# q and k of eight attention blocks read as pairs of tokens, in an attention and expert kernel on one core

## The chip, the cores and the metric

The kernel runs on one core of a Trainium2 chip. The core has a matrix engine (TensorE, PE in the profile; its weight loads are PEld), a vector engine (VectorE, DVE), an activation engine (ScalarE, ACT), a general engine (GpSimd, POOL), and SyncE (SP), which here only issues DMAs. Sixteen DMA engines move data between the device memory and the core's on-chip memory (SBUF); matrix results land in a second memory (PSUM), which DMAs don't reach. The metric is device time in microseconds of one launch. Before the change it was 397.56 us, the median of three runs (396.06 to 397.76).

## The reference

The kernel computes sliding-window attention with four sink tokens, and feeds the result to a layer of four experts that are all evaluated and mixed by given shares.

```python
# q, k, v: (4, 8, 768, 64) float32; n_sink = 4, window = 128
scores = q @ k.transpose / sqrt(64)
keep = (key < n_sink) | ((query - key >= 0) & (query - key < window))
a = softmax(where(keep, scores, -1e9))
x = (a @ v).transpose(0, 2, 1, 3).reshape(3072, 512)

p = domain_probs / (domain_probs.sum(-1) + 1e-9)        # (3072, 4), the shares
for e in range(4):                                      # w1: (4, 512, 1024), w2: (4, 1024, 512)
    out += p[:, e:e+1] * (relu(x @ w1[e]) @ w2[e])      # out: (3072, 512) float32
```

## The kernel before

Tokens are handled in 24 blocks of 128, each with all eight heads of one of the four sequences. Blocks 0 to 3 are the first 128 tokens of the four sequences, blocks 4 to 7 their second 128 tokens, and blocks 8 to 23 the rest, sequence by sequence. In the code a block is `u`; `place(u)` gives its sequence and its place in it.

A block is loaded by three DMAs on SP's queue (q, k, v; `load`, line 209). A DMA for 128 tokens and eight heads has 1024 pieces of 64 float32 numbers, 256 bytes each. Each of q, k and v has two buffers, so the load of block u waits until block u - 2 has been read. GpSimd casts what has landed to bf16 (`cast`, line 217). For blocks 0 to 7 TensorE transposes q and k (`pe_tr`, line 278); for blocks 0 and 1 it transposes the float32 numbers as they landed, without a cast. ScalarE or VectorE copies the transposed q and k out of PSUM (`q_out`, `k_out`). Later blocks are transposed by DMA. Keys of blocks 0 to 7 lie in the tile that all keys of a sequence share (sequences 0 and 1), or in a side tile `kside` (sequences 2 and 3), out of which `move_keys` copies them later. `sink_keys` copies the four sink keys of each sequence to tiles of their own, `skd`.

Then follow, for each block: the scores (`scores`, line 330: one matmul a head, 128 queries by the 128 keys of the block before and its own 128 keys, or its own alone in blocks 0 to 3); mask, scale and minimum on VectorE (line 353); exponentials on ScalarE (line 361); the transpose of the weights (tile `tra`, copied to `AT`); the product with v (`op`); the division by the sum (`xn`); and the transpose of the result to `xT`, the experts' input.

The experts' work is cut into items of tokens times one expert: first two items of 256 tokens (blocks 0 and 1, then 2 and 3) with expert 0, then items of 512 tokens. An item's first product goes to `hpsum` (line 494), passes a relu (`ht`) and its second product goes to `mopsum` (line 520). The result, times the token's share, is added into `out_sb`, and SP stores it (line 569). The eight weight tiles are loaded in pieces of 2 MB of float32 that the DMA casts to bf16, on GpSimd's own DMA queue (lines 228 and 231); the table `w_at` says behind which cast GpSimd issues each.

The shares are loaded as 24 rows of 2 KB, one row for each tile of 128 tokens, into `dp_nat` (`load_small`, line 234), the third DMA on SP's queue. TensorE turns them (`turn_shares`, tile `trs`, line 241), and VectorE divides them by their sums.

The order of all this is written out by a planner inside the kernel, which runs when the program is built. Each step is a node with engines and costs, dependencies and a due time (tables `starts` and `MOVED`); the planner always takes the step that can begin first and among these the one due first, and writes it to its engine. Each engine then works through its instructions strictly in that order, and waits where one is not ready. Where the planner sees TensorE without work in the first stage, it writes filler matmuls (`keep_busy`, line 478). SP's loads keep a fixed order. Each DMA of SP raises one of eight semaphores in turn, and so waits until the DMA eight places before it has landed.

Of the kernel before, what the change touches and what calls it, by code (L numbers as in the profile page):

```python
# [16 lines left out]
def kernel(  # L17
# [48 lines left out]
    UF = 2  # L66

# [23 lines left out]
    def tile_of(u):  # L91
# [17 lines left out]
    kside = {  # L109
        b: resid.tile([P, NHP, 2, P], BF16, name=f"kside{b}", tag=f"kside{b}") for b in range(2, B)  # L110
    }
# [23 lines left out]
    def own_keys(m):  # L135

        nc.gpsimd.affine_select(
            out=m, in_=m, compare_op=ALU.is_ge, fill=MASKED,
            base=0, pattern=[[-1, P]], channel_multiplier=1,
        )  # L140

    def keys_before(m):

        nc.gpsimd.affine_select(
            out=m, in_=m, compare_op=ALU.is_gt, fill=MASKED,
            base=0, pattern=[[1, P]], channel_multiplier=-1,
        )
# [3 lines left out]
    own_keys(M0)  # L151
    nc.vector.memset(M0[:, 0:NSINK], 0.0)
    for m in (M1, M2):
        nc.vector.memset(m, 0.0)
        own_keys(m[:, 1])
        keys_before(m[:, 0])
# [22 lines left out]
    def weigh_sinks(eng, u):  # L179
# [3 lines left out]
        for r in range(NSINK):  # L183
            t = sv if r == 0 else at_sb.tile([P, H, D], FP32, name="svr", tag="svr", bufs=1)
            nc.gpsimd.tensor_mul(  # L185
                t, vsb[place(u)[0]][:, :, r], pr[:, :, r : r + 1].to_broadcast([P, H, D])
            )
            if r:
                nc.gpsimd.tensor_add(sv, sv, t)  # L189
# [19 lines left out]
    def load(eng, u, what):  # L209
        b, qb = place(u)  # L210
        t = resid.tile([P, H, D], FP32, name="raw" + what, tag="raw" + what, bufs=NRAW[what])
        nc.sync.dma_start(  # L212
            out=t, in_=src_of[what][b, :, qb * P : (qb + 1) * P, :].rearrange("h p d -> p h d")
        )
        raw[what, u] = t

    def cast(eng, u, what):
# [5 lines left out]
        else:  # L223
            nat[what, u] = resid.tile([P, H, D], BF16, name=what + "n", tag=what + "n", bufs=2)
            copy_on(eng, nat[what, u], t)
# [29 lines left out]
    def keys_of(b):  # L255
        if b not in kT:
            kT[b] = at_sb.tile([P, NHP, NQB, P], BF16, name="kT", tag="kT", bufs=2)
# [5 lines left out]
    def front_keys(b):  # L263
        return kside[b] if b in kside else keys_of(b)
# [6 lines left out]
    def dma_k(eng, u):  # L271
        b, qb = place(u)
        nc.sync.dma_start_transpose(
            out=keys_of(b)[:, :, qb],
# [3 lines left out]
    def pe_tr(eng, u, what):  # L278
        src = raw.pop((what, u)) if u < UF else nat.pop((what, u))
        ps = ps_s.tile([P, NHP, P], FP32 if u < UF else BF16, name="tr" + what, tag="s")  # L280
        for hp in range(NHP):
            nc.tensor.transpose(  # L282
                ps[:, hp], src[:, 2 * hp : 2 * hp + 2, :], identf if u < UF else ident
            )
# [5 lines left out]
    def k_out(eng, u):  # L290
        b, qb = place(u)
        copy_on(eng, front_keys(b)[:, :, qb], live.pop(("trk", u)))

    def move_keys(eng, b):
        copy_on(eng, keys_of(b)[:, :, 1], kside[b][:, :, 1])
# [34 lines left out]
    def scores(eng, u, g):  # L330

        b, qb = place(u)
        lo = 0 if qb else 1
        kt = front_keys(b) if u < UPS else keys_of(b)
        first = qb - 1 + lo
        sp = {}
        for h in groups_of(u)[g]:
            if h % 2 not in sp:
                sp[h % 2] = ps_s.tile([P, 2, 2, P], FP32, name="sp", tag="s")
            r = slice(h % 2 * D, (h % 2 + 1) * D)  # L340
            nc.tensor.matmul(  # L341
                sp[h % 2][:, h // 2 % 2, lo:2], lhsT=queries_of(u)[r, h // 2],
                rhs=kt[r, h // 2, first : qb + 1], start=True, stop=True,
            )
# [221 lines left out]
    def store(eng, i, sub):  # L566
        tok = items[i][0] + sub * P
        rt = tile_of(tok // P)
        nc.sync.dma_start(
            out=out[rt * P : (rt + 1) * P, :], in_=out_sb[tok // 512][:, (tok % 512) // P, :]  # L570
        )
# [32 lines left out]
    starts = [-11.6, -24.6, 21.4, 5.8, 41.4, 66.5, 75.8, 38.7, 5.1, 34.6, 6.6, 66.0, 99.7]  # L604
# [17 lines left out]
    for u in range(NU):  # L622
# [4 lines left out]
        for j, what in enumerate("qkv"):  # L627
            last = u - NRAW[what]
            free = ("cast", last, what)
            if last < UF and what != "v":  # L630
                free = ("tr" + what, last)
# [5 lines left out]
            if u - AHEAD >= UPA:  # L637
                deps.append((("begun", "da", u - AHEAD, 1), HOP))
            node(("load", u, what), {"SP": 0.5}, lambda eng, u=u, w=what: load(eng, u, w), deps,
                 S0 - 24.0 + 0.1 * j, dma=1.0 if u < 2 else 1.1)  # L640
            deps = [(("load", u, what), HOP)]
            if u < UF and what != "v":
                continue
# [5 lines left out]
            elif u >= UF + 2:  # L649
# [413 lines left out]
```

## Time and profile before

| | |
|---|---|
| median of three runs | 397.56 us |
| the profiled execution | 396.68 us |
| its span, first to last instruction | 395.0 us |
| TensorE busy | 388.4 us |
| VectorE, ScalarE, GpSimd busy | 218.7, 213.7, 181.6 us |
| first expert matmul | 24.49 us after the span's start |
| filler matmuls on TensorE | 69 |
| packets of SP's DMA queue | 142724, 44.11 MB |
| packets of GpSimd's DMA queue (the weights) | 6272, 8.39 MB |

All times of instructions count from the span's start. The time of an execution is a little longer than its span. An engine's busy time is the time in which it had an instruction under way; a group's row gives how many instructions of a kind there were and how long one took on average. Matmuls overlap, so the step from one matmul's start to the next one's is shorter than the time of one: 0.216 us for 512 columns at the full clock, where one takes 0.379. The granted clock is the share of TensorE's clock that the chip let through. The share of the DMA engines can exceed 1, because packets on one engine overlap.

### The profile page before, as it was taken

Reading aid. Unit: us, or ns where it says so; the run is one execution under the profiler, and the core shown is the slowest. Engines: PE = TensorE matmul, PEld = TensorE weight load, DVE = VectorE, ACT = ScalarE, POOL = GpSimd, SP = SyncE. Lnnn points to the kernel's source line nnn. Section 1 sums busy time; section 2 is a strip of 40 time slices with the busy share of each in tenths; the row PEclk is TensorE's granted clock in tenths of the full one; section 3 lists DMA queues with packets and bytes.
Section 4 is the critical chain, followed back from the end, with each engine's and each line's share of the span. In section 5 each row is a group of like instructions: output and inputs, shape, how many; then the busy total and the mean of one; then the engine's idle time right before and its main releaser. Section 6 shows DMA issues by size and latency. Waiting matters only on the chain.

```text
span 395.0 us, 7130 instructions
## 1 busy us (share of the span) xinstructions
PE 388.4 (98%) x2457; PEld 193.2 (49%) x2457; DVE 218.7 (55%) x694; ACT 213.7 (54%) x606; POOL 181.6 (46%) x208
## 2 busy tenths in 40 slices
PE   7999999999999999999999999999999999999996
PEld 5776555544544444444444444444444444444443
DVE  2970678887355984943787934838845223101223
ACT  5875777667374563854564855835654342344320
POOL 2710332047828658595586981695975200000000
PEclk9989999999999999999999999999999999999999
DMA  9999999779299898795886948984933000110002
GB/s 177 211 200 199 205 205 183 185 116 194 57 138 201 178 228 204 139 210 99 196 163 148 209 99 166 217 140 84 217 95 69 13 2 0 53 55 0 0 2 106
DMA packets 149031, 52.94 MB, mean 134 GB/s; under 512 B 135404, under 2 KB 143980, under 8 KB 148996
## 3 DMA queue, kind: packets, MB, share of 16 engines
q1 hardware_dynamic: 142724, 44.11, 55.2%
q0 software_dynamic: 6272, 8.39, 13.3%
q8 instruction: 19, 0.31, 0.3%
q14 instruction: 16, 0.13, 0.1%
HBM read 39.90 MB, written 6.29 MB: 117 GB/s over the span
## 4 chain that ended last, share of the span: by engine, by line
PE 95%; DVE 2%; DMA 1%; SPq 1%; issue 0%
PE hpsum L494 43%; PE mopsum L520 42%; PE sp L341 3%; PE op L420 3%; PE tra L399 2%; DMA rawq<-in_q_dram 1%; PE idle_out L481 1%; DVE SM L353 1%; PE trq L282 1%; PE trk L282 1%; PE trx L470 1%; PE lpsum L537 0%; SPq L212 0%; PE ss L305 0%; SPq L234 0%
## 5 line engine op out<-in xcount | busy, mean ns | idle before, releaser
L494 PE MATMUL hpsum<-xT,w 128*128 128x512 bf16 (+1 forms) x800 | 180.6, 372 | 0.1
L520 PE MATMUL mopsum<-w,ht 128*128 128x512 bf16 x760 | 172.5, 379 | 0.0
L508 ACT ACTIVATE ht<-hpsum 128x512 bf16<-128x512 f32 x157 | 92.4, 595 | 99.8 <-PE hpsum L494 68.6
L520 PEld LDWEIGHTS <-ht 128*128 128x128 bf16 x760 | 73.3, 98 | 85.9 <-issue 0.6
L494 PEld LDWEIGHTS <-w 128*128 128x128 bf16 x800 | 74.6, 98 | 81.8 <-issue 9.1
L361 ACT ACTIVATE A<-SM,negm 128x256 bf16<-128x256 f32 (+1 forms) x192 | 91.7, 480 | 20.3 <-DVE negm L353 14.9
L562 DVE SCALAR_TENSOR_TENSOR out_sb<-mopsum,shares,out_sb 128x512 f32<-128x512 f32 x71 | 53.0, 746 | 81.1 <-PE mopsum L520 80.3
L189 POOL TENSOR_TENSOR sv<-sv,svr 128x512 f32<-128x512 f32 x48 | 60.9, 1269 | 3.8
L353 DVE CUSTOM_DVE_ANT_0 SM<-sp,M,slow 128x256 f32<-128x256 f32 x128 | 54.4, 478 | 6.7 <-PE sp L341 6.7
L185 POOL TENSOR_TENSOR svr<-vsb,As 128x512 f32<-128x512 f32 x48 | 52.9, 1102 | 2.5
L361 ACT ACTIVATION_READ_ACCUMULATOR A<-SM,negm 128x1 f32 x192 | 36.2, 188 | 0.0
L506 DVE TENSOR_SCALAR ht<-hpsum 128x512 bf16<-128x512 f32 x35 | 24.0, 686 | 16.6 <-PE mopsum L520 16.1
L558 ACT ACTIVATE out_sb<-mopsum,shares 128x512 f32<-128x512 f32 x20 | 13.8, 688 | 33.8 <-PE mopsum L520 33.8
L185 POOL TENSOR_TENSOR sv<-vsb,As 128x512 f32<-128x512 f32 x16 | 17.2, 1077 | 30.8 <-ACT As L375 30.8
L199 POOL CAST qn<-rawq 128x512 bf16<-128x512 f32 x22 | 13.5, 614 | 36.5 <-DMA rawq<-in_q_dram 35.0
L199 POOL CAST kn<-rawk 128x512 bf16<-128x512 f32 x22 | 13.6, 617 | 21.5 <-DMA rawk<-in_k_dram 17.5
L353 DVE CUSTOM_DVE_ANT_0 SM<-sp,M 128x128 f32<-128x128 f32 (+1 forms) x64 | 19.3, 352 | 5.8 <-PE sp L341 5.5
L448 DVE TENSOR_TENSOR sv<-op,sv 128x512 f32<-128x512 f32 x16 | 10.9, 683 | 20.2 <-POOL sv L189 17.7
L199 POOL CAST vn<-rawv 128x512 bf16<-128x512 f32 x20 | 13.2, 662 | 15.4 <-DMA rawv<-in_v_dram 15.4
L420 PEld LDWEIGHTS <-AT 128*128 128x128 bf16 x352 | 13.9, 100 | 4.8 <-issue 0.2
L353 DVE DVE_READ_ACCUMULATOR2_ANT negm<- 128x1 f32 x192 | 15.8, 82 | 0.0
L420 PE MATMUL op<-vn,AT 128*128 128x64 bf16 x288 | 14.4, 196 | 0.0
(79 smaller groups left out, 197.9 us busy)
## 6 DMA issues: line engine op xcount, KB each, us to landing
w<-in_moe_w_dram POOLq DMA_DIRECT2D x8, 1024.0 KB, 11.4
rawq<-in_q_dram SPq DMA_DIRECT2D x24, 256.0 KB, 3.7
rawk<-in_k_dram SPq DMA_DIRECT2D x24, 256.0 KB, 5.0
rawv<-in_v_dram SPq DMA_DIRECT2D x24, 256.0 KB, 5.4
out_dram<-out_sb SPq DMA_DIRECT2D x23, 256.0 KB, 2.4
vsb<-in_v_dram SPq DMA_DIRECT2D x4, 1024.0 KB, 7.0
AT<-A SPq DMA_TRANSPOSE x32, 4.2
qT<-qn SPq DMA_TRANSPOSE x16, 2.5
```

The source lines that it names most:

```text
L185: nc.gpsimd.tensor_mul(t, vsb[place(u)[0]][:, :, r], pr[:, :, r : r + 1].to_broadcast([P, H, D]))
L189: nc.gpsimd.tensor_add(sv, sv, t)
L199: nc.gpsimd.tensor_copy(out=out, in_=in_)
L353: nc.vector.tensor_tensor_reduce(out=SM[:, h][part], in0=live.pop(("sp", u, h))[part], in1=masks[min(qb, 2)], scale=-scale, scalar=live["s ...
L361: nc.scalar.activation(out=Abuf[u % 2][:, 2 * h + lo : 2 * h + 2, :], in_=SM[:, h, lo:2], func=AF.Exp, scale=-1.0, bias=live["negm", u][:, ...
L420: nc.tensor.matmul(op[:, h], lhsT=at[:, 2 * h + i], rhs=vn[key][:, h, :], start=(i == blocks[0][0]), stop=(i == 1),)
L494: nc.tensor.matmul(ps[:, j * n : (j + 1) * n], lhsT=w1[e][:, db, fb * P : (fb + 1) * P], rhs=xT[t0 // 512][:, db, t0 % 512 : t0 % 512 + n] ...
L506: nc.vector.tensor_scalar_max(out=ht, in0=ps, scalar1=0.0)
L508: nc.scalar.activation(out=ht, in_=ps, func=AF.Relu)
L520: nc.tensor.matmul(ps, lhsT=hidden(i, fb, sub), rhs=w2[e][:, fb, :], start=(fb == 0), stop=(fb == NFB - 1),)
L558: nc.scalar.activation(out=dst, in_=ps, func=AF.Copy, scale=sc)
L562: nc.vector.scalar_tensor_tensor(out=dst, in0=ps, scalar=sc, in1=dst, op0=ALU.mult, op1=ALU.add)
```

## The change

Of blocks 0 to 7, q and k are read as pairs of tokens. Two tokens that follow each other in a sequence are 512 adjacent bytes for one head. A load is now two DMAs, one for heads 0 to 3 and one for heads 4 to 7, each of 64 token pairs times four heads: the pair's number and the group of heads give the partition, so that the first DMA fills the even partitions and the second the odd ones. v is read as before.

After the cast and the transpose, a head's 128 tokens lie in every second column of a tile of 256, first the even tokens and then the odd ones. Queries stay in this order: rows of a block are then tokens 0, 2, 4, ..., 1, 3, 5, .... Masks of these blocks are set up for it in two halves, stores are two DMAs of 64 rows each, and the shares of these eight tiles are read once more, in eight small DMAs, into the order of the rows. Keys are read in the order of the tokens, alternately out of the even and the odd half. All keys of blocks 0 to 7 stay in `kside`, now one tile for each sequence, and `move_keys` falls away. Where a block's keys lie in `kside`, or in `kside` and in the tile of the later keys, its scores take two matmuls of 128 keys for each head instead of one of 256.

Blocks 0 and 1 are now cast too, by VectorE, and no block is transposed in float32. The shares are loaded behind v of block 3. The table of the weights, the planner's due times and some of its costs are new, so that the order of the instructions changes on every engine: there are 105 fillers instead of 69, the shares are turned after the first 24 expert matmuls instead of before them, and in GpSimd's order the first three weight pieces are issued behind the casts of k of block 2 (two pieces) and of v of block 3.

```diff
     def load(eng, u, what):
...
+        from_ = src_of[what][b, :, qb * P : (qb + 1) * P, :]
+        if u < UPS and what != "v":
+            for g in range(2):
+                nc.sync.dma_start(
+                    out=t.rearrange("p (f j) d -> p f (j d)", j=2)[g::2, 0:NHP],
+                    in_=from_[g * NHP : (g + 1) * NHP].rearrange("f (p j) d -> p f (j d)", j=2),
+                )
+        else:
+            nc.sync.dma_start(out=t, in_=from_.rearrange("h p d -> p h d"))
...
     def cast(eng, u, what):
...
+            if u < UPS:
+                copy_on(
+                    eng, nat[what, u].rearrange("p (j f) d -> p f j d", j=2),
+                    t.rearrange("p (f j) d -> p f j d", j=2),
+                )
...
+    def load_pairs(eng):
+        for b in range(B):
+            for j in range(2):
+                nc.sync.dma_start(
+                    out=dp_nat[b * NQB : b * NQB + 2, j * D : (j + 1) * D],
+                    in_=moe_domain_probs[b * S : b * S + 2 * P].rearrange(
+                        "(t p j) e -> j t p e", t=2, j=2
+                    )[j],
+                )
...
+    def front_queries(u, h):
+        t = qTb[u % 2].rearrange("p (m j) c -> p m (j c)", j=2)
+        r = slice(h % 2 * D, (h % 2 + 1) * D)
+        return t[r, h % NHP // 2, h // NHP :: 2]
+
+    def front_keys(b, qb, h):
+        r = slice(h % 2 * D, (h % 2 + 1) * D)
+        return kside[b][r, h % NHP // 2, qb].rearrange("p (j c) -> p c j", j=2)[:, h // NHP :: 2]
...
     def sink_keys(eng, b):
         for c in range(2):
             r = slice(c * D, (c + 1) * D)
-            copy_on(eng, skd[b][r, :, c], front_keys(b)[r, :, 0, 0:NSINK])
+            for g in range(2):
+                copy_on(
+                    eng, skd[b][r, g * HG : (g + 1) * HG, c].rearrange("p m (j t) -> p m j t", j=2),
+                    kside[b][r, :, 0].rearrange("p m (j c) -> p m j c", j=2)[:, :, :, g : g + 3 : 2],
+                )
...
     def scores(eng, u, g):
         b, qb = place(u)
...
+        parts = [(0, 2)] if qb > 2 else [(0, 1), (1, 2)] if qb else [(1, 2)]
...
+            for a, z in parts:
+                if qb - 1 + a < 2:
+                    keys = front_keys(b, qb - 1 + a, h)
+                else:
+                    keys = keys_of(b)[r, h // 2, qb - 3 + a : qb - 3 + z]
+                nc.tensor.matmul(
+                    sp[h % 2][:, h // 2 % 2, a:z],
+                    lhsT=front_queries(u, h) if u < UPS else queries_of(u)[r, h // 2],
+                    rhs=keys, start=True, stop=True,
+                )
...
     def store(eng, i, sub):
...
+        for j in range(2):
+            nc.sync.dma_start(
+                out=rows.rearrange("(p j) d -> j p d", j=2)[j], in_=have[j * D : (j + 1) * D]
+            )
...
-            node(("cast", u, what), {"POOL": 0.56},
+            node(("cast", u, what), {"DVE": 0.42} if u < 2 and what != "v" else {"POOL": 0.62},
...
-    w_at = [(2, 'k'), (2, 'k'), (2, 'k'), (4, 'q'), (5, 'q'), (6, 'k'), (9, 'v'), (11, 'q')]
+    w_at = [(2, 'k'), (2, 'k'), (3, 'k'), (4, 'k'), (5, 'v'), (6, 'v'), (9, 'k'), (9, 'v')]
...
+    node(("pairs",), {"SP": 4.0}, load_pairs, [], 5.0, dma=0.9)
-    node(("trs",), {"PE": 0.46}, turn_shares, [(("small",), HOP), (("s", 3, 1), 0.0)], 9.0, "s")
+    node(("trs",), {"PE": 0.46}, turn_shares, on([("pairs",), ("s", 3, 3)]), 9.0, "s")
...
-        if u == 0:
-            loads.insert(2, ("small",))
+        if u == 3:
+            loads += [("small",), ("pairs",)]
```

More of the change, by code (lines that the diff above doesn't have):

```diff
@@ L64 @@
     UG = 4
-    UF = 2
     NVN = 4
@@ L108 @@
     skd = [resid.tile([P, NHP, 2, NSINK], BF16, name=f"skd{b}", tag=f"skd{b}") for b in range(B)]
-    kside = {
-        b: resid.tile([P, NHP, 2, P], BF16, name=f"kside{b}", tag=f"kside{b}") for b in range(2, B)
-    }
+    HG = H // NHP
+    kside = [
+        resid.tile([P, HG, 2, HG * P], BF16, name=f"kside{b}", tag=f"kside{b}") for b in range(B)
+    ]
     idle_in = consts.tile([P, P], BF16, name="idle_in")
@@ L278, in pe_tr @@
     def pe_tr(eng, u, what):
[L279 to L284, printed above, removed]
+        src = nat.pop((what, u))
+        ps = ps_s.tile([P, NHP, P], BF16, name="tr" + what, tag="s")
+        for j in range(2):
+            for m in range(HG):
+                i = j * HG + m
+                nc.tensor.transpose(ps[:, m * 2 + j], src[:, 2 * i : 2 * i + 2, :], ident)
         live["tr" + what, u] = ps
@@ L568, in store @@
         rt = tile_of(tok // P)
-        nc.sync.dma_start(
-            out=out[rt * P : (rt + 1) * P, :], in_=out_sb[tok // 512][:, (tok % 512) // P, :]
-        )
+        rows, have = out[rt * P : (rt + 1) * P, :], out_sb[tok // 512][:, (tok % 512) // P, :]
+        if tok // P >= UPS:
+            nc.sync.dma_start(out=rows, in_=have)
+            return
+        for j in range(2):
+            nc.sync.dma_start(
+                out=rows.rearrange("(p j) d -> j p d", j=2)[j], in_=have[j * D : (j + 1) * D]
+            )
     nodes = {}
@@ L674 @@
                 have.append((("dk", u - 1), HOP))
-            elif b >= 2:
-                node(("kc", b), {"POOL": 0.56, "ACT": 0.58}, lambda eng, b=b: move_keys(eng, b),
-                     kfree + on([("ko", B + b)]), S0 - 6.0)
-                have.append((("kc", b), HOP))
             else:
```

118 lines of the change are left out of this document (51 added, 67 removed).

## The prediction

> **What bounds the kernel now.** I read the page's busy times and the chain first, then busy times by stage, then the packets of the DMA queues by stage, then the timelines of PE and POOL.
>
> ```profile
> PE 388.4 (98%) x2457; PEld 193.2 (49%) x2457; DVE 218.7 (55%) x694; ACT 213.7 (54%) x606; POOL 181.6 (46%) x208
> PE 95%; DVE 2%; DMA 1%; SPq 1%; issue 0%
> ```
>
> TensorE is busy throughout, and the chain runs over it for 95% of the span. So an edit counts only as it moves the start of the steady stretch, adds matmul time, or makes PE wait.
>
> ```profile
> 5.00:10.00 5.00, 4.25 (x24) 2.88 (x23) 1.88 (x13) 3.59 (x15) 0.61 (x1) 1.00 1.33 221
> 15.00:20.00 5.00, 4.55 (x60) 3.61 (x57) 4.73 (x23) 4.14 (x22) 3.57 (x6) 1.00 1.17 204
> 20.00:25.00 5.00, 4.65 (x48) 3.52 (x49) 4.77 (x33) 4.89 (x25) 0.39 (x2) 0.80 1.17 199
> 30.00:35.00 5.00, 5.00 (x41) 3.77 (x39) 0.00 (x0) 2.98 (x5) 0.00 (x0) 1.00 1.13 203
> ```
>
> Columns: stage, its length, busy PE, PEld, DVE, ACT, POOL, granted clock, DMA share, GB/s. Until about 24 us the attention of blocks 0 to 3 runs: DVE is at 4.7 of 5 us, ACT at 4.1 to 4.9, the DMA engines are full. PE's busy time there holds 69 filler matmuls. From 24.5 us on PE has no gap.
>
> ```profile
> 22.74 0.67 PE L241 MATMUL trs<-identf,dp_nat 24*128 24x24 f32 x4
> 23.34 0.29 PE L481 MATMUL idle_out<-idle_in 128*128 128x128 bf16 x1
> ...
> 13.09 0.61 POOL L199 CAST kn<-rawk 128x512 bf16<-128x512 f32 x1 [0.44 <-DMA rawk<-in_k_dram]
> 13.64 0.94 POOL L228 DMA_DIRECT2D w<-in_moe_w_dram  x1
> ```
>
> The turn of the shares (trs) stands in PE's order just before the first expert matmul (24.49 us). The weights start behind the cast of k of block 2.
>
> ```profile
> q1 hardware_dynamic: 7808, 1.97, 131.4%
> ...
> q0 software_dynamic: 267, 0.54, 95.4%
> q1 hardware_dynamic: 265, 0.07, 17.4%
> ...
> q0 software_dynamic: 461, 0.47, 92.2%
> q1 hardware_dynamic: 458, 0.12, 29.5%
> ```
>
> These are queue lines (packets, MB, share) of 5 to 14 us, 30 to 33 us (first weights, 2 KB pieces) and 24 to 27 us (second weights, 1 KB). Alone, the loads move 868 packets of 256 B per us: 16 engines / 868 = 18.4 ns each on one engine, 1.18 us a load. Beside weights the two queues take **turns, packet for packet**: 267 to 265, 461 to 458. One turn of both costs an engine 48 us / 267 = 180 ns, or 48 / 461 = 104 ns. A small packet then waits for a big one each time.
>
> **The change, part by part.** All against the profiled execution, 396.68 us (span 395.0); it lies 0.9 below the median, 397.56, within the runs' 396.06 to 397.76.
>
> *Loads.* A q or k load becomes two DMAs of 256 packets of 512 B. The packet records have 27 ns for the 512 B pieces of the last stores, 18 for 256 B: 512 x 27 / 16 = 0.86 us against 1.18. Block 3's k, the eighth such load, landed at 16.6 us; 8 x 0.3 earlier, and 0.7 more for the share load that leaves the head of the queue, is 13.5. SP issues 20 DMAs for four blocks instead of 12. One with 128 rows took 0.33 to 0.57 us, a DMA transpose 1.2; I take 0.45, nearest in kind: 2.3 us a block, under the 2.9 of its transfers. At 1.2 SP would be the bound, 5 us a block, +7 in all.
>
> *Blocks 0 and 1.* Four casts on DVE replace float32 transposes. Four transposes took 1.09 us in float32 and 0.59 in bf16; the cast lies between 0.41 (DVE bf16 copy) and 0.69 (float32 to bf16); I take 0.42, since it reads SBUF. Per load that is nothing net on the chain, but DVE gets 1.7 us more; the copies out of bf16 take 0.42 there instead of 0.69. The sink-key copies double (0.41 to about 0.8 us a block; block 2's on ACT, the others on POOL). ACT's own front (32 exps at 0.39, seven copies, the sink keys: 17 us from 7.7 us) then ends about 24: ACT and not the loads sets the end, so the first expert matmul comes at about 24.0 instead of 24.5. Term: **-0.5** (from -3.1, if it followed block 3's k, to +1, if the 105 fillers, 36 more, run at the slow 0.107 us).
>
> *Scores.* 64 score matmuls of 256 columns in the steady stretch become 128 of 128 with two weight loads a head. Eight heads took 0.45 us from first start to last plus its pitch, two heads side by side. Half-width ones of one head cannot run side by side: five steps of 0.056 for four heads against 0.225. Eight blocks x 2 groups x 0.06 = **+1.0** (0.4 to 3.6, if none overlap). The moving keys are now read alternating between two runs 256 B apart; no row of before has such a read; bounds are 0 and a doubled 0.056 step. The Trainium skill ("SBUF — State Buffer", section on Door 1) says that reads crossing to a new 16-byte line each time pay a penalty, and these do; it gives no figure, and at double steps the sum would have +4.9 here instead of +1.0. I stay at 1.0, since no row shows the penalty.
>
> *Shares.* This is the large term. The share load (before: second on the queue, 24 rows of 2 KB) now follows block 3's v, and eight more DMAs rewrite parts of dp_nat. Each has 2 rows of 64 pieces of 16 B. They wait for the first one (same tile), and trs, in PE's order 2.84 us after the first expert matmul (sum of the pitches ahead of it), waits for all. An engine takes whole rows: the landing record of before's 24-row load has 12 arrivals, that of every 128-row load 16. Two rows thus use two engines at most, 64 packets on each, 512 for the eight. The Trainium skill ("DMA: Bandwidth & Descriptors", section on why a DMA increments its semaphore by 16) says the same: the largest count up to 16 that divides the slowest dimension, and always the lowest-numbered engines; the 12 of 24 rows agrees.
>
> Block 3's v lands near 14.6, so the pair loads start near 15 to 16. The weights come first: k of block 2 lands near 10.6, POOL has its sink copies and q's cast ahead of it and ends k's cast near 12.0, so w starts 1.6 us earlier than 13.64. In before three pieces went out back to back and the third landed at 36.4 us, 22.75 after the first issue; now 34.5, its last packet at 33.5. They are 32 + 64 + 32 turns per engine, some 120 of them after 16 us, and each lets one pair packet through. So at 33.5 two engines still hold 512 - 120 = 392. Alone each costs between 0 and 18.4 ns (the 256 B row): 0 to 7.2 us; I take 9 ns, half, since 16 B are less than 256: 3.6. Landing takes about 1 us more (first load: 3.3 us from issue, its packets done after 2.3). Landed: **38.1** (34.5 to 41.7). PE stands at trs from 24.0 + 2.84 = 26.8: **+11.3** (7.7 to 14.9). Everything on PE queues behind it; so do SP's next loads, since each waits for the eighth DMA before it to land. They then have no weights beside them and come 8 us or more before PE needs q of block 4 (8.5 us of expert work comes first), so I cost them nothing; if that cover fails, the trk of block 5 is late next, 18 us after trs.
>
> *Clock.* Before shows one spell at half clock: 0.80 and 0.86 over 20 to 30 us, 1.7 us lost. An idle PE of 11 us should bring one more: **+1.7** (0 to 3.4).
>
> *The rest.* Stores of eight tiles are cut in two: 8 more DMAs, 0.33 to 0.53 us each on SP, beside PE's steady work. Two key moves (0.6 us) go. POOL's casts keep 0.61. Three more mask steps (0.29 each) end before the first load lands. Nothing on the path; if SP were late, the AT transposes would be next.
>
> Sum: 396.7 - 0.5 + 1.0 + 11.3 + 1.7 = 410.2; against the median, half of the 0.9 added, **411**.
>
> **Rivals.**
> - *The pair loads are hidden and the front follows the loads.* If the sixteen engines shared the 1024 pieces, 64 each, they would be through at 16 + 24 turns of 180 ns + 40 of 104 = 24.5 us, landed before 26.8: no wait. Fourteen engines are the point from which this decides; the 12 arrivals speak against. With the first expert matmul 3.1 us sooner: 396.7 - 3.1 + 1.0 = 394.6. For it: DMA is full until 24 us. Against: DVE and ACT are at 4.7 and 4.1 of 5 us.
> - *Hidden, and ACT sets the front's end:* 396.7 - 0.5 + 1.0 = 397.2, no change that can be told.
> - *Hidden, but PE's new key reads run at half pace:* 396.7 - 0.5 + 4.9 = 401.1. Nothing in the profile speaks for or against.
>
> **Numbers.** Forecast 0.66, by the turns (two stretches, 1 to 1) and the 12 arrivals; first rival 0.10, second 0.13, third 0.11. Own range of the forecast: 405 (wait 8, no clock spell) to 417 (wait 15, clock 3.4, scores 2), the other terms as taken. To leave out no more than 2 in 10, the range goes down to 397, which takes in the third rival and half of the second: 397 to 418. About 0.5% (2 us) is what a measurement of this kernel tells from no change: faster 0.10, same 0.13, slower 0.77.
>
> **What the profile after will show.** PE idle of 8 to 15 us ending in trs, with dp_nat's DMA as its releaser, near 27 to 39 us; DMA share falling to a small part once the weights are through; the loads of block 4 issued late; a half-clock spell after 38 us; first expert matmul near 24; score steps of 0.056. Wrong would make it: dp_nat landed before 26 us (pieces over all engines, or queues that don't take turns), or weights that start after the pair loads.

## The result

The changed kernel takes 413.79 us, median of four runs (412.38 to 414.26), beside 396.81 (395.47 to 397.76, four runs) for the kernel before on the same chip. The ratio is 1.0419, 95% interval 1.0368 to 1.0471: slower by 17.0 us. Forecast were 411 us, 405 to 417 for the likeliest case, and 397 to 418 with the rivals. One execution of an experiment below (the turn put later) ran at a granted clock of 0.66 and took 575 us; it stands in no median here. The profiled execution took 414.26 us, its span is 412.5 us. The page's busy times and chain:

```profile
PE 390.0 (95%) x2515; PEld 196.6 (48%) x2557; DVE 206.5 (50%) x683; ACT 223.1 (54%) x620; POOL 180.9 (44%) x218
...
PE 88%; DMA 5%; SPq 4%; issue 1%; DVE 1%; ACT 0%; DVEq 0%; ACTq 0%
```

TensorE is still the bound, but 9% of the chain are now DMAs and SP's issue of them (before: 1% and 1%). PE's waits (tile and line, its releaser: us in all, times, longest) and the timelines of PE, SP and GpSimd say where:

```profile
PE trs L267 <- DMA dp_nat<-in_moe_domain_probs_dram: 10.9, 1, 10.9
PE hpsum L534 <- DMA xT<-xn: 1.5, 1, 1.5
```

```profile
25.68 1.04 PE L534 MATMUL hpsum<-xT,w 128*128 128x256 bf16 x8
...
39.91 0.64 PE L267 MATMUL trs<-identf,dp_nat 24*128 24x24 f32 x4 [10.88 <-DMA dp_nat<-in_moe_domain_probs_dram]
...
40.88 6.99 PE L534 MATMUL hpsum<-xT,w 128*128 128x256 bf16 x40
```

```profile
13.70 0.56 SPq L224 DMA_DIRECT2D rawv<-in_v_dram  x1
14.31 0.58 SPq L250 DMA_DIRECT2D dp_nat<-in_moe_domain_probs_dram  x1
27.33 10.43 SPq L257 DMA_DIRECT2D dp_nat<-in_moe_domain_probs_dram  x8
```

```profile
13.47 0.94 POOL L244 DMA_DIRECT2D w<-in_moe_w_dram  x1
...
26.95 0.61 POOL L203 CAST vn<-rawv 128x512 bf16<-128x512 f32 x1 [9.94 <-DMA rawv<-in_v_dram]
```

PE stood at the turn of the shares from 29.0 to 39.9 us, and started again at half clock (the stage's columns as in the prediction; the eighth number is the granted clock):

```profile
40.00:45.00 5.00, 5.00 (x28) 3.77 (x29) 1.00 (x4) 1.64 (x3) 2.66 (x4) 0.50 0.80 212
```

The 40 expert matmuls from 40.88 took 6.99 us; the first 23 of them stepped by 0.213 us, the 24th by 0.173, the others by 0.109. The pair loads were issued only from 27.33 us: v of block 3, which SP issued 0.2 us after GpSimd had issued the first weight piece, landed at 26.9, and the 24-row load behind it, for which the pair loads wait, at 27.3. The queues of 30 to 33 us, when PE waited (queue: packets, MB, share):

```profile
q0 software_dynamic: 271, 0.56, 103.8%
q1 hardware_dynamic: 35, 0.00, 1.6%
```

271 weight packets on sixteen engines are 16.9 for each. 35 pair packets on two engines are 17.5 for each: turns, packet for packet, on two engines. Until 34.8 us the pair packets went two to four in 0.2 us, from then on up to 68, so that from there these two engines seem to have had no weight packets left (the third piece landed at 36.5). 912 of the 1024 pair packets, 456 an engine, were still to go, and went in 4.3 us: 253 from 35 to 36 us, then some 200 per us, as fast as SP issued them (128 in 0.64 us).

The score matmuls between 52 and 75 us that read keys out of `kside` (ns min/median/max, start of the first and last, form), first before (blocks 6 and 7), then after (blocks 4 to 6, without the last two matmuls):

```profile
L341 PE MATMUL sp<-kside,qT x16: 266/269/280, 61.2 to 70.2; 64*128 64x256 bf16 x16
```

```profile
L380 PE MATMUL sp<-kside,qT x46: 296/298/304, 56.0 to 75.0; 64*128 64x128 bf16 x46
```

A matmul of half the keys takes longer than one of all had. By the starts in the trace, two heads side by side step, from pair to pair, by 0.137 us for 128 alternating keys; in block 8, whose second half comes out of the tile of the later keys, they step by 0.057 for 128 keys in a row. (From the second head of a pair to the next pair it is 0.130 and 0.050.)

The books, span against span (17.5 us): the first expert matmul comes 1.2 later (25.68, before 24.49); the wait 10.9; score matmuls, start to next start, 15.65 after and 11.50 before, 4.15; half-clock steps 2.7 after and 1.0 before, 1.7; the wait for xT 1.5; the turns, now behind the first expert matmul, 0.6. That is 20.1. Against it, the 512-column matmuls of the experts lost less than before: over 0.216 us for each, those of the first products took 3.3 us before and 1.2 after (the wait for xT aside), those of the second 0.6 and 0.1, 2.6 less in all (with 42 matmuls whose records are missing after counted at 0.216): 17.5. Why they lost less is not shown.

### The profile page after: what moved, and what is told of

The parts are those of the page before. It is cut to its first block, busy times and chain, and to the rows that moved or that the text cites. A ratio compares the mean times of both kernels' runs of the same rounds, so it can differ in the third digit from the quotient of the medians.

```text
span 412.5 us, 7404 instructions
## 1 busy us (share of the span) xinstructions
PE 390.0 (95%) x2515; PEld 196.6 (48%) x2557; DVE 206.5 (50%) x683; ACT 223.1 (54%) x620; POOL 180.9 (44%) x218
## 3 DMA queue, kind: packets, MB, share of 16 engines
HBM read 39.91 MB, written 6.29 MB: 112 GB/s over the span
## 4 chain that ended last, share of the span: by engine, by line
PE 88%; DMA 5%; SPq 4%; issue 1%; DVE 1%; ACT 0%; DVEq 0%; ACTq 0%
PE hpsum L534 39%; PE mopsum L560 39%; PE sp L380 4%; DMA dp_nat<-in_moe_domain_probs_dram 4%; SPq L257 2%; PE op L460 2%; PE tra L439 1%; SPq L219 1%; DMA rawq<-in_q_dram 1%; DMA xT<-xn 1%; PE lpsum L577 0%; DVE SM L393 0%; PE trx L510 0%; PE trq L316 0%; PE ss L341 0%
## 5 line engine op out<-in xcount | busy, mean ns | idle before, releaser
L534 PE MATMUL hpsum<-xT,w 128*128 128x512 bf16 (+1 forms) x773 | 184.3, 375 | 3.0 <-DMA xT<-xn 1.5
L560 PE MATMUL mopsum<-w,ht 128*128 128x512 bf16 x745 | 176.3, 379 | 0.8 <-issue 0.2
L548 ACT ACTIVATE ht<-hpsum 128x512 bf16<-128x512 f32 x173 | 102.8, 595 | 116.1 <-PE hpsum L534 102.7
L534 PEld LDWEIGHTS <-w 128*128 128x128 bf16 x800 | 76.2, 99 | 82.4 <-issue 5.0
L401 ACT ACTIVATE A<-SM,negm 128x256 bf16<-128x256 f32 (+1 forms) x192 | 91.9, 481 | 22.1 <-DVE negm L393 16.9
L189 POOL TENSOR_TENSOR svr<-vsb,As 128x512 f32<-128x512 f32 x48 | 51.5, 1073 | 2.5
L203 POOL CAST vn<-rawv 128x512 bf16<-128x512 f32 x20 | 12.3, 613 | 21.2 <-DMA rawv<-in_v_dram 20.7
L598 ACT ACTIVATE out_sb<-mopsum,shares 128x512 f32<-128x512 f32 x17 | 11.7, 688 | 17.0 <-PE mopsum L560 15.8
L350 DVE TENSOR_SCALAR sneg<-ss 128x32 f32<-128x32 f32 x16 | 3.0, 185 | 30.0 <-PE ss L341 30.0
L488 DVE TENSOR_TENSOR sv<-op,sv 128x512 f32<-128x512 f32 x16 | 10.9, 684 | 12.0 <-PE hpsum L534 6.6
L380 PEld LDWEIGHTS <-qT 64*128 64x128 bf16 x256 | 10.8, 95 | 11.3 <-issue 8.3
```

The lines of the kernel that those rows point to most:

```text
L189: nc.gpsimd.tensor_mul(t, vsb[place(u)[0]][:, :, r], pr[:, :, r % 2 * 2 + r // 2][:, :, None].to_broadcast([P, H, D]))
L203: nc.gpsimd.tensor_copy(out=out, in_=in_)
L380: nc.tensor.matmul(sp[h % 2][:, h // 2 % 2, a:z], lhsT=front_queries(u, h) if u < UPS else queries_of(u)[r, h // 2], rhs=keys, start=True, ...
L401: nc.scalar.activation(out=Abuf[u % 2][:, 2 * h + lo : 2 * h + 2, :], in_=SM[:, h, lo:2], func=AF.Exp, scale=-1.0, bias=live["negm", u][:, ...
L534: nc.tensor.matmul(ps[:, j * n : (j + 1) * n], lhsT=w1[e][:, db, fb * P : (fb + 1) * P], rhs=xT[t0 // 512][:, db, t0 % 512 : t0 % 512 + n] ...
L548: nc.scalar.activation(out=ht, in_=ps, func=AF.Relu)
```

## The experiments

Each kernel changes the changed kernel in what its diff shows, or stands on another experiment where the text says so; the ratio is to the kernel before in the same comparison.

### The pair loads taken away

```diff
+    def part_pairs(eng):
+        copy_on(eng, dp_two, dp_nat.rearrange("t (c j) e -> t j c e", j=2))
...
             nc.tensor.transpose(ps[:, e, 0:NTB], dp_nat[:, :, e], identf[0:NTB, 0:NTB])
+            nc.tensor.transpose(
+                ps[:, e, NTB : 2 * NTB], dp_two.rearrange("t j c e -> t (j c) e")[:, :, e],
+                identf[0:NTB, 0:NTB],
+            )
...
-            loads += [("small",), ("pairs",)]
+            loads += [("small",)]
```

> The changed kernel without the eight pair loads: the 24 rows of the shares are loaded where the changed kernel loads them (behind v of block 3), VectorE copies them once in even, odd order (24 x 512 float32), and TensorE turns both copies in the place where the changed kernel turns one. Theory (the 10.9 us of PE before trs are the pair loads' own): the first load of the shares landed at 27.3 us, PE reaches trs near 29.0, so the wait falls under 1 us, and with it goes the half-clock spell after it (24 expert matmuls at 0.213 instead of 0.109 us, and the turns, 2.7 us); four more turns cost 0.5. 414.3 - 10.9 - 2.7 + 0.5 = 401.2 us (399.5 to 403). Rival (the weights and v of block 3 hold the stage up, and the wait only moves to the next loads or to w): a wait of 4 us or more at another tile between 27 and 45 us, 404 to 410. Second rival (the clock spell comes from the early stage and not from the idle time): the wait goes, the spell stays, 403.9.

Measured: 401.34 us (401.24 to 402.64), ratio 1.0107 (1.0023 to 1.019); 12.4 us less than the changed kernel. Its timelines of VectorE and PE:

```profile
28.23 0.40 DVE L202 COPY dp_two<-dp_nat 24x512 f32<-24x512 f32 x1
...
30.64 0.29 PE L271 MATMUL trs<-identf,dp_nat 24*128 24x24 f32 x1
```

The turn (here behind 32 expert matmuls, not 24) stands without a wait, and every step between two expert matmuls around it is 0.109 us: with the idle time went the half clock. Both rivals fall. The pair loads were the cost. Four more turns on PE, 0.5 us, and 1.05 us of VectorE do their work: the copy shown, and five copies out of PSUM (0.26 and 0.39 us) that pick the rows.

### The weights issued later

```diff
-    w_at = [(2, 'k'), (2, 'k'), (3, 'k'), (4, 'k'), ...
+    w_at = [(3, 'v'), (3, 'v'), (3, 'v'), (4, 'k'), ...
```

> The changed kernel with the first three weight pieces issued behind the cast of v of block 3 instead of behind k of block 2 (two) and v of block 3 (one). Theory (the pair loads are slow since their start and their packets take turns with the weights): without weights beside them v of block 3 lands near 15.5 us, the 24-row load near 17, and the eight pair loads are then paced by SP's issue, 0.6 to 0.7 us each, and land near 22 to 23: under 7 us from first issue to last landing instead of 12. No wait for dp_nat on PE. The weights start 2 to 3 us later, so w sets the first expert matmul, near 27 instead of 25.7. 414.3 - 10.9 - 2.7 + 1.3 = 402 us (400 to 405). Rival (two engines are slow on 16-byte pieces by themselves, whatever lies beside them): 10 us or more from first issue to last landing, PE waits for dp_nat until 27 to 30 us; 403 to 407.

Measured: 418.0 us (417.41 to 419.26), ratio 1.0519 (1.0445 to 1.0593): slower yet, and neither forecast. v of block 3 landed by 18.4 and the share load by 17.5 us (forecast: 15.5 and 17); but eight issues take SP 5 us, the weights were issued from 18.93, and only 358 pair packets, less than three of the eight loads, went before the weights' first ones. Queue q1 (here the pair packets) from 19 to 20 us, without weights, and both queues from 30 to 33:

```profile
q1 hardware_dynamic: 222, 0.00, 12.0%
...
q0 software_dynamic: 561, 0.62, 121.6%
q1 hardware_dynamic: 68, 0.00, 3.1%
```

```profile
40.09 0.64 PE L267 MATMUL trs<-identf,dp_nat 24*128 24x24 f32 x4 [13.98 <-DMA dp_nat<-in_moe_domain_probs_dram]
```

The same packets on the same two engines: 222 per us alone, 23 per us beside weights (68 / 2 = 34 an engine, 561 / 16 = 35). So two engines are not slow by themselves, which the rival had said; the turns make them so, and the end follows that of the weights, whose third piece landed at 39.45 us. That the time is 4 us worse than the changed kernel's fits the planner's order: here trs stands ahead of the first expert matmul, which came at 42.90, so that the second products begin at 51.13 us and not at 47.71.

### The turn put later

```diff
-    ... turn_shares, on([("pairs",), ("s", 3, 3)]), 9.0, "s")
+    ... turn_shares, on([("pairs",), ("mm2", 0, 1)]), 9.0, "s")
```

> The changed kernel with the pair loads untouched and trs put behind the second product of the first item (64 expert matmuls and two times eight second products may go before it). Theory (PE loses time only because trs stands where it does, and what is late next is q of block 4, whose loads are issued behind the pair loads): PE works on until about 37.4 us, then waits in trq of block 4, whose cast ended at 42.5 us in the changed kernel, and not in trs: some 4.8 us instead of 10.9. 414.3 - 6.1 - 1 (a shorter half-clock spell) = 407 us (405.5 to 409). Rival A (a reader of the on-record text: the later loads have 8 us of cover and cost nothing): PE waits for dp_nat alone, 2 to 2.5 us, 404. Rival B (the wait just moves along with trs): 413 or more.

> The kernel of e5_turns_later once more, for a trace at the full clock. As there: theory, a wait of some 4.8 us for q of block 4 and 407 us; rival A, a wait of 2 to 2.5 us for dp_nat alone and 404 us; rival B, 413 or more.

Measured: 405.8 us (404.82 to 408.81, three runs), ratio 1.0262 (1.021 to 1.0314). Again: 407.0 (406.75 to 407.26, two runs), ratio 1.0261 (1.0202 to 1.032), as the theory said. PE's longest wait in the second (the 4.6 us hold another of 0.7 at 57.5 us):

```profile
PE trq L316 <- POOL qn L203: 4.6, 2, 3.9
```

PE does not wait for dp_nat any more. It waits for q of block 4 until 42.26 us, 3.9 us, and then finds the shares there. So the loads behind the pair loads are next in line, and rival A falls with the prediction's 8 us of cover, as soon as the first wait is mended: PE has used up the expert work by then.

### How the keys are read

Keys in two runs, and keys put in a row by the copy out of PSUM:

```diff
-        return kside[b][r, h % NHP // 2, qb].rearrange("p (j c) -> p c j", j=2)[:, h // NHP :: 2]
+        return kside[b][r, h % NHP // 2, qb].rearrange("p (j c) -> p j c", j=2)[:, :, h // NHP :: 2]
```

```diff
-            eng, kside[b][:, :, qb],
-            live.pop(("trk", u)).rearrange("p (m j) c -> p m (j c)", j=2),
+            eng, kside[b][:, :, :, qb].rearrange("p m g (f j) -> p m g f j", j=2),
+            live.pop(("trk", u)).rearrange("p (m j) (f g) -> p m g f j", j=2, g=2),
...
-        parts = [(0, 2)] if qb > 2 else [(0, 1), (1, 2)] if qb else [(1, 2)]
+        parts = [(0, 1), (1, 2)] if qb == 2 else [(0, 2)] if qb else [(1, 2)]
```

> The changed kernel with the keys of blocks 0 to 7 read first from the even and then from the odd stretch, each with a step of two elements, instead of alternately from both; the keys then stand in another order than the masks, so the scores of blocks 0 to 8, 12, 16 and 20 are not the reference's. All else is the same. In the changed kernel a pair of 128-key matmuls (two heads side by side) steps by 0.137 us where the keys alternate and by 0.050 where they lie in a row (blocks 8, 12, 16, 20). Theory A (the alternation between places 256 bytes apart is what costs): the steps fall to about 0.055, sixteen matmuls of a block from 1.20 to 0.6 us, and the time by 3 us, 411.3. Theory B (any step over neighbours costs the same): steps of 0.13 stay, and 414.3. Theory C (it is the crossing to another 16-byte line: a step of 4 bytes crosses at every fourth element): steps between 0.055 and 0.09.

> The changed kernel with the keys of blocks 0 to 7 put in the order of the tokens by the copy out of PSUM (the copy reads alternately, 512 elements, and writes in a row); blocks 4 to 7 have one matmul of 256 keys for each head again, blocks 8, 12, 16 and 20 still two of 128. Theory (the reads and the split cost 4.1 us in the steady stretch): blocks 4 to 7 go from 1.2 to 1.3 us each back to 0.65, the other four lose 0.17 each: 414.3 - 4 x 0.63 - 4 x 0.17 = 411.1 us (410.2 to 412). The copies may take 0.6 instead of 0.43 us; the front may end up to 1 us later, which the wait for the shares hides (it ends at 39.9 either way). Rival (score matmuls are hidden or made up elsewhere in the steady stretch): 413.5 to 414.5. Second rival (the copies hold the front up by more than 3.3 us, over what the wait hides): over 412.

Measured: 409.22 us (one execution; it leaves out the right order of the keys) and 409.49 (408.5 to 410.52), the second with ratio 1.0301 (1.0227 to 1.0375). Score matmuls between 52 and 75 us out of `kside`, in two runs and in a row:

```profile
L380 PE MATMUL sp<-kside,qT x48: 214/215/230, 54.5 to 71.8; 64*128 64x128 bf16 x48
```

```profile
L380 PE MATMUL sp<-kside,qT x24: 269/269/281, 53.9 to 71.1; 64*128 64x256 bf16 x24
```

Theory A: with a step of two elements, but one run after the other, a pair of heads steps by 0.058 us again, and a block's sixteen matmuls take 0.57 us instead of 1.20. It is the alternation and not the step of 4 bytes that costs: with the step alone the pair is as fast as with keys in a row. All score matmuls behind the first expert matmul add up to 11.94 and 11.58 us, against 15.65 in the changed kernel and 11.50 before; so alternation cost 3.7 us, and the split into two matmuls at most 0.4. In the profiled executions (409.22 and 408.5, against 414.26) most of the rest is an earlier end of the wait (39.00 and 37.81 us instead of 39.91): v of block 3 and the share load just meet the weights, and the pair loads were issued from 25.31 and 25.23 us instead of 27.33. By the medians e4 gained 4.3 us, and not the 3.2 forecast with the wait's end left in its place.

### Who casts block 1

```diff
-            node(("cast", u, what), {"DVE": 0.42} if u < 2 and what != "v" else {"POOL": 0.62},
+            node(("cast", u, what), {"DVE": 0.42} if u < 1 and what != "v" else {"POOL": 0.62},
```

> e1_shares_on_chip with q and k of block 1 cast by GpSimd instead of VectorE; block 0 stays on VectorE. In the changed kernel VectorE waited 1.27 us for q of block 1 (until 8.35 us) with the minima of block 0, which had their scores since 7.8, behind it in its order; the first exponential came at 9.02 instead of 7.98 us before, and ScalarE then ran almost without a gap to 25.75. Theory (this wait sets the first expert matmul, because ScalarE is the bound of the early stage): first exponential near 8.0, ScalarE's last one of block 3 and the first expert matmul 1.0 us earlier than in e1 (26.5 there), 401.3 - 1.0 = 400.3 us (399.5 to 401). Rival (the loads, issued one every 0.62 us, set the stage's end): first expert matmul within 0.3 us of e1's, 401.3. Second rival (GpSimd's cast of block 1 behind its sink copies is later than VectorE's): first expert matmul later than in e1, 401.5 to 402.5.

On top of e1. Measured: 401.77 us (401.67 to 405.04), ratio 1.0164 (1.0122 to 1.0206): no gain over e1's 401.34. The mechanism did show: first exponential at 7.97 us, first expert matmul at 25.05 instead of 26.48. But the gain was given back. A wait of PE in the profiled execution, at 405.04 the slowest of the four:

```profile
PE mopsum L575 <- DMA w<-in_moe_w_dram: 1.9, 1, 1.9
```

The second products reached w2 of the first expert before it had landed, at 32.62 us (31.42 in e1), and a new half-clock spell came with this wait (granted clock 0.50 from 31.8 to 38.6 us). That is seen in this execution only. What made w2 land later is not shown, and why the other three, at 401.7, gained nothing either stays open.

### All together, and two ways to miss

> All three together: shares turned out of one load (now behind v of block 1, the copy in even, odd order on GpSimd, turned before the first expert matmul), keys in the order of the tokens, block 1 cast by GpSimd. The 512-byte loads, the even, odd queries and the split stores stay. Theory (the terms add up): 401.3 for e1, -4.0 for the keys (e4 against the changed kernel, 4.3, less the part that lies in the early stage), -1.0 for the cast, -0.9 for turns that fill PE's free time: 395.4 us (394 to 397.5), the kernel before within a measurement. Rival (the early stage gets longer with the slower key copies on VectorE, 0.69 instead of 0.42 us): 396.5 to 399. Second rival (the 512-byte loads do bring the early stage forward once nothing stands in the way): first expert matmul under 23.5 us, 393 or less.

> e7_shares_keys_cast with block 1 cast by VectorE as in the changed kernel, and the planner's cost of issuing a q or k load put from 0.9 to the measured 1.27 us (two DMAs), of another from 0.5 to 0.6, so that it orders VectorE's work by the real landing times; nothing else is set. Theory (the order and not the engine of the cast is what delayed the exponentials): the first four minima of block 0 go ahead of the cast of block 1's q, first exponential near 8.0 us, and the time as e7's within 1.5 us: 394.5 to 397. Rival (two casts on VectorE, the nearly full engine, cost the early stage 0.85 us more): 1 us or more over e7.

e7 is e1 with e4's and e6's edits, the share load behind v of block 1, the copy on GpSimd, and the planner's cost of the scores of blocks 4 to 7 as in one matmul; e8 takes e6's edit back and sets `{"SP": 1.27 if pairs else 0.6}`. Measured: 398.13 us (397.27 to 400.79), ratio 1.0054 (1.003 to 1.0079), and 406.68 (404.24 to 407.1), ratio 1.0255 (1.0219 to 1.029). Both missed their forecasts, e7 by under 1 us and e8 by 10 us. Their longest waits of PE:

```profile
PE trk L331 <- POOL kn L204: 2.0, 1, 2.0
```

```profile
PE trk L331 <- POOL kn L204: 4.1, 1, 4.1
```

With one more DMA ahead of it (the share load, 0.65 us on SP), it is now k of block 3 that meets the weights: its second DMA was issued at 13.66 and 14.66 us, the first weight piece at 14.07 and 14.00. Its cast came at 20.11 and 23.76 us instead of 16.39, and the first expert matmul at 29.1 and 31.3. First exponentials came at 8.86 and 8.97, so the order that I meant to get did not come about either. Some half a microsecond on SP cost several here, where it put a load beside the weights' first packets. The rest of e8's 8.5 us over e7 was not taken apart.

### One DMA for each load

```diff
-            for g in range(2):
-                nc.sync.dma_start(
-                    out=t.rearrange("p (f j) d -> p f (j d)", j=2)[g::2, 0:NHP],
-                    in_=from_[g * NHP : (g + 1) * NHP].rearrange("f (p j) d -> p f (j d)", j=2),
-                )
+            nc.sync.dma_start(
+                out=t.rearrange("p (f j) d -> p f (j d)", j=2)[:, 0:NHP],
+                in_=from_.rearrange("(g f) (p j) d -> p g f (j d)", g=2, j=2),
+            )
```

> The changed kernel with each q or k load of blocks 0 to 7 as one DMA of 128 rows instead of two of 64; the 512 pieces of 512 bytes are the same. Theory (SP's issue, 0.62 us a DMA, 13.7 us for 20 of them, paced the early loads and made v of block 3 and the share load meet the weights): 12 DMAs take SP under 8 us, the transfers pace, v of block 3 is issued before 11 us and lands before 16 instead of 26.9, the pair loads are issued from 16 to 17 us instead of 27.3. They get some 200 packets per us until the weights begin, about 20 beside them, and end 1 to 2 us after the three weight pieces, which start 1 us earlier: trs near 36.5 to 38 instead of 39.9. 413.8 - 2.5 = 411.3 us (409.5 to 413). Rival (the wait is set by the first share load's and v's landing, not by the weights' end): with both 10 us earlier the pair loads end by 28, no wait, 401. Second rival (the issue does not pace): nothing moves, 413.8.

Measured: 411.36 us (409.16 to 412.51), ratio 1.0364 (1.0313 to 1.0415). SP's timeline and the turn:

```profile
1.66 0.63 SPq L218 DMA_DIRECT2D rawk<-in_k_dram  x1
...
11.14 0.63 SPq L223 DMA_DIRECT2D rawv<-in_v_dram  x1
...
16.19 18.06 SPq L256 DMA_DIRECT2D dp_nat<-in_moe_domain_probs_dram  x8
```

```profile
36.35 0.64 PE L266 MATMUL trs<-identf,dp_nat 24*128 24x24 f32 x4 [7.62 <-DMA dp_nat<-in_moe_domain_probs_dram]
```

The queues from 28 to 31 us:

```profile
q0 software_dynamic: 306, 0.62, 110.5%
q1 hardware_dynamic: 39, 0.00, 1.8%
```

A DMA of 128 rows costs SP what one of 64 costs, 0.62 us. v of block 3 was cast at 16.46 us (26.95 with two DMAs), the pair loads were issued from 16.19, and still PE waited until 36.35: the loads began 11 us sooner and ended 3.6 us sooner, as the third weight piece landed 3.8 us sooner (32.70 us instead of 36.46). By 31.8 us, when the pair packets became fast, only 198 of the 1024 had gone: 39 in these three microseconds, 19.5 an engine, beside 306 / 16 = 19.1 of the weights. This is the course that the prediction had described, with its own starting times, and the rival that the landing of the first share load decides falls.

> e1_shares_on_chip and e4_keys_in_order together: no pair loads, and the keys in the order of the tokens; all else as in the changed kernel. Theory (the two causes are separate and add up): e1 took 12.4 us off the changed kernel, e4 4.3, of which 1.7 was an earlier end of the wait that e1 no longer has: 413.8 - 12.4 - 3.2 = 398 us (396.5 to 399). What is then left of the change (512-byte loads, even and odd order, split stores) is worth nothing or costs 1 us against the kernel before, 396.5. Rival (one of the two gains was the other's): 400 or more.

> e9_shares_and_keys with one DMA for each q or k load. Theory (with the shares and the keys mended, the faster loads are free to act, and q of block 1 lands before VectorE needs it): first exponential near 8.0 instead of 9.0 us, first expert matmul 1 us earlier, 398 - 1 = 397 us (395.5 to 398.5), no change against the kernel before that can be told. Rival (the early stage really was waiting for loads): first expert matmul 3 us earlier than in e9, 395 or less. Second rival (w1 or w2 of the first expert becomes the bound as soon as the rest is faster, since the loads of block 4 now share the DMA engines with them earlier): no gain over e9.

e9 (e1 with e4's edit): 398.12 us (397.56 to 400.04, ten runs), ratio 1.0047 (1.002 to 1.0074). e11 (the same with one DMA a load): 396.0 (395.19 to 396.47, ten runs), ratio 0.9972 (0.9942 to 1.0001), against 396.97 for the kernel before. Taken off one after the other, by the medians, the pair loads are worth 12.4 us, the keys 3.2 and the second DMA of each load 2.1: 17.7, which leaves nothing of the 17.0 that the change cost (e11's median lies 0.97 below that of before). Alone, the keys brought 4.3 us and the single DMA 2.4, so what one repair is worth depends somewhat on the others. First exponential and first expert matmul of e11:

```profile
8.32 0.40 ACT L415 ACTIVATE A<-SM,negm 128x128 bf16<-128x128 f32 x1 [2.27 <-DVE negm L407]
```

```profile
24.02 1.04 PE L548 MATMUL hpsum<-xT,w 128*128 128x256 bf16 x8
```

They lie at 9.04 and 25.82 in e9. With all repairs the 512-byte loads bring the first expert matmul 0.5 us forward against before, and the time is, within what can be told, that of the kernel before; the interval ends at 1.0001.

## Why the prediction was right, and where not

*Shares, +11.3 predicted, 10.9 measured.* Right, by its mechanism: two engines, turns one to one with the weights, a rest that goes fast once they are through (4.3 us for 456 packets an engine; the text had 3.6 for 392), PE queued behind trs. e1, e2 and e10 show each part. Each pair load's landing record has two arrivals, besides one right after its issue (the last load's: 39.42 and 39.45 us). Yet three steps failed and nearly cancelled. "The pair loads start near 15 to 16" failed: they started at 27.3, because v of block 3 itself met the weights. The weights were not 1.6 us earlier than before but 0.2 (13.47 us), and the third piece landed at 36.5 and not at 34.5. That moved the landing little, since the end follows the weights' end and not the start: 39.4 instead of 38.1. And PE arrived at 29.0 instead of 26.8. That 10.9 came out so near 11.3 is in part luck. The Trainium skill's rule ("DMA: Bandwidth & Descriptors", section on why a DMA increments its semaphore by 16), the number of engines by the slowest dimension, agrees: in the three stretches counted above and below (35 to 271, 68 to 561 in e2, and 39 to 306 in e10) the turns come out one to one only for two engines.

*Loads.* "I take 0.45" for an issue on SP failed: it was 0.60 to 0.62 us. Five DMAs a block then take 3.35 us and not 2.3, more than the 2.9 of their transfers, so SP paced the early loads and not the DMA engines (their share was 0.89 to 1.00 in the three stages from 5 to 20 us, before 1.17 to 1.33), and v of block 3, the twentieth DMA, went out at 13.70. The bound of 1.2 had been priced (five DMAs of 1.2 us are 6 us a block, not the text's 5), the value between, from which SP decides, had not. e9 against e11 gives it: 2.1 us. (The share load had been third on SP's queue, not second, which changes nothing in the sum.)

*Blocks 0 and 1, -0.5 predicted, +1.2 measured.* "Nothing net on the chain" failed. VectorE works in order, and the cast of block 1's q, which waited for its load until 8.35 us, stood ahead of the minima of block 0:

```profile
8.35 0.43 DVE L201 CAST qn<-rawq 128x512 bf16<-128x512 f32 x1 [1.27 <-DMA rawq<-in_q_dram]
```

The first exponentials, before and after:

```profile
7.98 0.40 ACT L361 ACTIVATE A<-SM,negm 128x128 bf16<-128x128 f32 x1 [0.28 <-DVE negm L353]
```

```profile
9.02 0.40 ACT L401 ACTIVATE A<-SM,negm 128x128 bf16<-128x128 f32 x1 [2.53 <-DVE negm L393]
```

ScalarE, which does set the end of the early stage, passed this microsecond on; in e6, without that cast on VectorE, the first exponential came at 7.97 us and the first expert matmul 1.4 us sooner than in e1. The text's own sum has 17 us from 7.7, which is 24.7 and not "about 24". I had counted the cast's time and not what queues behind its wait. Where loads come sooner (e11), the term is the -0.5 of the text.

*Scores, +1.0 predicted, 4.15 measured,* above the upper bound of 3.6. Both halves were wrong. The split costs at most 0.4, because two heads still run side by side. The alternating reads, put at nothing, cost 3.7: a step of 0.137 instead of 0.057 us. The rule of the Trainium skill that I had weighed and set aside ("SBUF — State Buffer", section on Door 1: full pace needs two reads or more of one 16-byte line) was right in direction. The text's +4.9 was nearer; by its own steps it would have been +5.4 if all double, +4.3 if only the alternating ones do. e3 agrees with it in detail too: a step of 4 bytes, four reads to a line, costs nothing that shows (0.058 us). The third rival had this mechanism, but only with the shares hidden; the two came together.

*Clock, +1.7 predicted, +1.7 measured:* a new spell of 2.7 us behind the wait, while the early one's 1.0 us no longer fell on expert work. It goes with the wait: the granted clock was 0.50 from 32.3 to 45.9 us here, for 3.4 us behind the 3.9 us of waiting in e5, and 1.00 from 18.4 us to the end in e1 and from 17.3 us in e9.

*The rest.* Nothing was to be on the path; the wait of 1.5 us for xT, until 166.4 us, was. It is in the changed kernel, e3, e4 and e10 and in none of the others. What makes it late I did not find out. The 8 us of cover for block 4's loads held here (its trq had no wait at 51.16 us), but not once trs had gone on (e5).

The first two rivals fell with dp_nat's landing. The sum came out within 3 us, and that was in part luck: a term that was 3.2 too small for the scores, one 1.7 too small for the early stage and a wait of 1.5 left out stood against 2.6 us that the experts' matmuls lost less than before, and the large term came out right from a wrong start.

## What to carry to other kernels

A small transfer on few engines, beside large ones on the same engines, ended here when the large ones ended, although it started 11 us earlier in e10; what is only a change of order was better done on chip (1.05 us of VectorE and 0.5 of PE, against 12.4). Count DMAs as well as bytes: two of half the size cost the issuing engine twice, and a load that this pushes behind the first packets of a long transfer was late here by ten microseconds. Read a moving operand in runs, and put data in order in the copy that is there anyway.

## What the runs showed that I had not expected

- A q or k DMA costs SP 0.60 to 0.62 us to issue in the changed kernel's early stage (the very first one 0.79), and one of 128 rows of 2 KB in e10 0.60 to 0.63 where SP does not wait; the two DMAs of one load cost 1.26 us.
- A matmul whose moving operand alternates between two places 256 bytes apart steps 2.4 times as slowly (0.137 against 0.057 us for 128 columns of two heads); a step of two bf16 elements inside a run costs nothing.
- The copy that puts the keys in order reads PSUM alternately. It took VectorE 0.689 us instead of 0.423, and ScalarE 0.588 instead of 0.587.
- 16-byte packets of two engines went at some 200 to 280 per us alone, and at some 10 to 25 per us beside weight packets of 1 to 2 KB.
